# Another order from the planner, and another way to fetch alpha, in a fused attention and two-MLP kernel

## Chip, cores and metric

The kernel runs on one core of a Trainium2 chip, in one launch. The metric is device time in microseconds (us). The engines are named as in the profile: PE (TensorE), PEld (its weight loads), DVE (VectorE), ACT (ScalarE), POOL (GpSimd) and SP (SyncE), which here issues every DMA.

## What is computed

Attention with a forget gate over 4 batches, 8 heads, 576 positions and a head width of 64, then two MLPs over the 2304 resulting rows (512 to 2048 to 512 each). The reference, cut to what matters:

```python
cum = np.cumsum(np.log(np.clip(f, 0.0001, 1.0)), axis=-1)
scores = scale * q @ k.T + (cum[..., :, None] - cum[..., None, :])   # causal
attn = softmax(scores) ; x = attn @ v        # -> (2304, 512)
h = x @ w_in
g = np.maximum(h, 0.0) + alpha * np.minimum(h, 0.0)                  # first MLP
x = g @ w_out
h = x @ moe2_w_in
g = np.maximum(h, 0.0) + np.log1p(np.exp(-np.abs(h)))                # second MLP
return g @ moe2_w_out
```

`alpha` has one number for each of the 2048 hidden columns.

## The kernel before

**The work.** Two heads of one batch make a pair; there are 16 pairs. A pair is worked in nine query tiles (four of each head, and one with the last 64 rows of both). For a tile, POOL writes the decay into `d`, PE writes scores into PSUM (`pt`, L621 or L634), DVE adds them and takes the row maximum (L643), ACT takes the exponential into `p` (L651), PE turns `p` over (L660), ACT and DVE split the result into a high and a low part (L681, L685), and PE multiplies it with the values (L725). `row_sums` sends the row sums by way of DRAM (`rd`, L781) and back as a broadcast (`rb`, L786, L790).

**The MLPs** are split into items of 384 rows (a chunk) by 512 hidden columns. Each item has four times `hidden` (12 matmuls, L889, and the nonlinearity on ACT and DVE, with `slope` holding minus alpha at L902) and the `product` (12 matmuls in each of four groups, L946). Each weight block is fetched raw, 512 KB in 64-bit words (`raw`, L386 and L391), and taken apart by ACT and DVE in eight steps that begin with `ca` on ACT (L394); blocks that are needed again are saved to DRAM (`w_dh`, `w_dl`, L438).

**Stages.** The first eight pairs run with twice the buffers and PE has no MLP work beside them. Then `switch1` gives half of the space to the first MLP: its twelve items on chunks 0 to 2 are mixed with pairs 8 to 15. The rows of those pairs go to DRAM (`xb_dh`, `xb_dl`, L817) and come back after `switch2` as chunks 3 to 5 (`x3h`, `x3l` and so on, L849). From there on PE has only MLP work.

**What sets the order.** Every step is given to `Plan` with an engine, a length, what it reads and writes, and a rank. `Plan.emit` plays the steps through with these lengths and, whenever an engine is free, takes the ready step of the lowest rank. The order in which it takes them is the order in which the instructions are written; on the chip each engine then goes through its own list in that order and waits where an operand is not there. So the lengths only decide the order, and an error in them shows as a wait. `hop` is the allowance from one engine to the next, `late` what a transfer adds to the transfer clock, and `TUNE` has the offsets of the ranks, in steps of a query tile or of an MLP block: two numbers for a step of the attention (first and second eight pairs), one for a step of the MLPs.

Of the kernel before, what the change touches and what calls it, by code (L numbers as in the profile page):

```python
# [14 lines left out]
ALU = mybir.AluOpType  # L15
# [3 lines left out]


TUNE = {
    "TILE1": 0.42, "TILE2": 0.47, "SLOT2": 7.65, "SLOT3": 13.68, "qr": (-5.98, -0.1), "kr": (0.68, -0.52),
    "vr": (-1.32, 560.85), "cum": (11.69, 8.14), "q": (-1.09, -699.23), "k": (-3.93, -2.73),
    "v": (8.47, 0.66), "decay": (-1.18, 0.77), "scores": (0.88, 3.13), "max": (-8.47, 0.3),
    "pad": (-25.9, 9.39), "exp": (79.74, 1.39), "turn": (-0.12, -0.34), "hi": (1.38, 0.0),
    "lo": (2.49, -2.45), "values0": (16.5, 0.87), "values1": (148.3, 515.38), "sum": (3.42, -0.84),
    "finish": (-1.52, 37.07), "sums": (-1.34, -5.25), "blocks": 6.2, "product": 14.59, "total": 1.13,
    "weights": -0.99, "raw": -0.0, "mlp": -1.66,
}


class Plan:
# [7 lines left out]
    @staticmethod  # L40
    def hop(a, b):

        if a == b:
            return {"pe": 0.0, "dve": 0.13}.get(a, 0.1)
        if b == "act":
            return 0.2
        return {"pe": 0.11, "pool": 0.17, "dve": 0.29 if a == "pe" else 0.15}.get(b, 0.1)
# [33 lines left out]
    def emit(self):  # L81
        ops, place = self.ops, self.place
# [47 lines left out]
        while done < len(ops):  # L130
            moved = True
            while moved:
                moved = False
                for e in engines:
                    if free[e] > now + 1e-9:
                        continue
                    best, got = None, None
                    for n in waiting[e]:
                        if ops[n][9] and port_at > now + 1e-9:
                            continue  # L140
                        if can[n] <= now + self.LOOK and (best is None or ops[n][5] < ops[best][5]):
                            g = get_room(n)
                            if g is not None:
                                best, got = n, g
                    if best is None or can[best] > now + 1e-9:
                        continue
                    waiting[e].remove(best)
                    for key, x in got.items():
                        place[key] = x
                        room[key[0]].remove(x)  # L150
                        for line in (key[0], key[:2]):
                            if line in self.queue:
                                served[line] += 1
                    free[e] = now + ops[best][1]
                    end = free[e]
                    if ops[best][9]:
                        port_at = end
                    if e == "sp":
                        moved_at = max(now + 1.2, moved_at) + ops[best][6]
                        moved_at = max(moved_at, end + 0.6 + ops[best][6] / 2)  # L160
                        end = moved_at + 0.95
                    running.append((end, best))
                    order.append(best)
                    moved = True
            times = [t for t, _ in running] + [can[n] for e in engines for n in waiting[e] if can[n] > now + 1e-9]
            times += [t for t in (port_at, *free.values()) if t > now + 1e-9]
            assert times, [sorted([(ops[n][5], ops[n][4]) for n in waiting[e]], key=str)[:3] for e in engines]
            now = min(times + [t for t, _ in leaving])
            for t, key in [x for x in leaving if x[0] <= now + 1e-9]:
                leaving.remove((t, key))  # L170
                room[key[0]].append(place[key])
            for t, n in [r for r in running if r[0] <= now + 1e-9]:
                running.remove((t, n))
                done += 1
                for tag, ids in (ops[n][7] or {}).items():
                    room[tag].extend(ids)
                for key in uses[n]:
                    pending[key] -= 1
                    if not pending[key]:
                        leaving.append((t + 0.2, key))  # L180
                for m in after[n]:
                    left[m] -= 1
                    hop = 0.0 if ops[n][0] == "sp" else self.hop(ops[n][0], ops[m][0])
                    can[m] = max(can.get(m, 0.0), t + hop)
                    if not left[m]:
                        waiting[ops[m][0]].append(m)
# [30 lines left out]
def forgetting_attention_two_mlps(  # L217
# [18 lines left out]
    nc = tc.nc  # L236
# [12 lines left out]
    NFF = DFF // 128  # L249
# [5 lines left out]
    NU = len(UNITS)  # L255
    SWITCH = len(pairs) // 2

    plan = Plan(
        {
            "qr": [0], "kr": [0], "vr": [0], "cumb": [0, 1], "q": [0], "k": [0], "qw": [0, 1], "kw": [0, 1], "v": [0, 1],  # L260
            "d": [0, 1, 2, 3], "p": [0, 1, 2, 3], "mx": [0, 1, 2, 3], "sm": [0, 1], "xt0": [0], "xt1": [0], "x32": [0, 1], "r": [0],
            "rd": [0, 1], "rb": [0], "pt": list(range(8)), "ahead": [0, 1, 2, 3],
            **{"P%d%d%d" % (t, x, n): [0] for t in range(len(UNITS)) for x in range(2) for n in range(2)},
            "raw": [0, 1], "ca": [0, 1], "cu": [0, 1], "win": list(range(5)),
            "wout": [], "h": [], "o": [], "g": [], "ta": [],
        },
# [7 lines left out]
    TILE1, TILE2, SLOT2, SLOT3 = (TUNE[x] for x in ("TILE1", "TILE2", "SLOT2", "SLOT3"))  # L274
    DUE = TUNE
    T_HALF = TILE1 * SWITCH * NU

    def R(n):

        return n * TILE1 if n < SWITCH * NU else T_HALF + (n - SWITCH * NU) * TILE2  # L280
# [15 lines left out]
    ident = const.tile([128, 128], F32, name="ident")  # L296
# [5 lines left out]
    slope = const.tile([128, NFF], F32, name="slope")  # L302
# [14 lines left out]
    def buf(key):  # L317
        return tiles[key[0], plan.place[key]]
# [43 lines left out]
    def weights(kind, m, ff, key, rank):  # L362
# [13 lines left out]
        rkey, ua, uu = ("raw", key), ("ca", key), ("cu", key)  # L376
# [43 lines left out]
            nc.vector.scalar_tensor_tensor(out=buf(key)[1], in0=buf(ua), scalar=2.0 ** -52, in1=buf(uu).bitcast(F32),  # L420
                                           op0=ALU.mult, op1=ALU.mult)

        plan.add("sp", 0.65, load, reads=[("begun", 1)], writes=[rkey], rank=rank + DUE["raw"], late=1.46)
        plan.add("act", t_act(512), lower, reads=[rkey], writes=[ua], rank=rank)
        plan.add("dve", t_dve(512, True), shift, reads=[ua], writes=[uu], rank=rank, port=True)
        plan.add("dve", t_dve(512), join, reads=[rkey], writes=[uu], rank=rank, port=True)
# [578 lines left out]
    with tc.manual_schedule():  # L1005
# [142 lines left out]

        for i in range(SWITCH):
            pair(i)  # L1150
        plan.add("sp", 0.5, lambda: nc.sync.dma_start(out=slope, in_=alpha.rearrange("(k p) -> p k", p=128)),
                 reads=[("y", 0, 0, 0)], writes=[("alpha",)], rank=60, late=0.2)
        plan.add("dve", 0.1, lambda: nc.vector.tensor_scalar(out=slope, in0=slope, scalar1=-1.0, scalar2=None, op0=ALU.mult),
                 writes=[("alpha",)], rank=60)

        plan.add("switch", 0.0, switch1, reads=plan.everything(), writes=[("switch1",)], rank=0.0,
                 grow={"wout": range(5), "g": range(6), "ta": range(2), "h": range(2), "o": range(2)})
# [54 lines left out]
```

## Time and profile before

| | |
|---|---|
| median of 3 runs | 1038.0 us (1037.36 to 1039.97) |
| time of the profiled execution | 1037.31 us |
| its span in the trace | 1035.1 us |
| busy in the span: PE, DVE, ACT, POOL | 1022.3, 725.1, 518.5, 240.3 us |
| HBM read and written | 78.66 MB, 22.17 MB |
| mean granted clock of TensorE | 0.995 of full |

The profiled execution's time is 2.2 us more than its span. PE's busy time counts overlapping matmuls once, so its gaps are real waits; but a busy PE may still be slowed, by a lower granted clock or by a short wait that the end of the matmul before covers.

### The profile page before, as it was taken

To read this page: it belongs to the slowest core of one execution; us is meant where nothing else is said; L and a number is where in the kernel's file an instruction comes from. 1 tells how busy PE (TensorE), PEld (TensorE's weight loads), DVE (VectorE), ACT (ScalarE), POOL (GpSimd) and SP (SyncE) were. 2 spreads that over 40 slices of the span, in tenths; PEclk is the share of its full clock that TensorE was granted. 3 is DMA by queue.
4 is the path that set the end of the run, shared out by engine and by line. 5 is a ranking of instruction groups with operands and counts; after the bars stand their busy time and mean duration, and the time that the engine had idled before them with its cause. 6 is when DMAs were issued, how large, how long until landed. Compare 5 with 4: busy or idle time off the path is not lost.

```text
span 1035.1 us, 17156 instructions
## 1 busy us (share of the span) xinstructions
PE 1022.3 (99%) x6023; PEld 946.4 (91%) x6023; DVE 725.1 (70%) x1605; ACT 518.5 (50%) x1264; POOL 240.3 (23%) x399
## 2 busy tenths in 40 slices
PE   8899999999999999999999999999999999999998
PEld 6678899999999899999999999999999998999997
DVE  5898789979999988532335488738765885685543
ACT  6778777776767655344333354434522332332221
POOL 7677766355566520000000000000000000000000
PEclk8999999999999999999999999999999999999999
DMA  7676446646654248020412221202110211010102
GB/s 185 158 225 176 106 124 198 196 147 184 198 167 144 92 159 288 18 71 32 142 40 84 82 61 34 69 1 82 39 45 1 82 41 42 1 41 1 61 31 91
DMA packets 114021, 101.94 MB, mean 98 GB/s; under 512 B 66624, under 2 KB 87248, under 8 KB 113936
## 3 DMA queue, kind: packets, MB, share of 16 engines
q1 hardware_dynamic: 113936, 100.86, 32.3%
q8 instruction: 47, 0.77, 0.3%
q14 instruction: 38, 0.31, 0.1%
HBM read 78.66 MB, written 22.17 MB: 97 GB/s over the span
## 4 chain that ended last, share of the span: by engine, by line
PE 81%; DVE 7%; ACT 4%; issue 3%; POOL 3%; DMA 2%; POOLq 0%; ACTq 0%; DVEq 0%; SPq 0%
PE o L946 36%; PE h L889 35%; PE pt L725 3%; PE pt L621 3%; PE pt L660 2%; POOL d L599 2%; ACT p L651 1%; PE pt L508 1%; DVE d L643 1%; DMA raw<-in_moe_w_in_dram 1%; PE pt L634 1%; DVE p01l L685 1%; DVE ca L409 1%; DVE g L928 1%; DVE acc L967 1%
## 5 line engine op out<-in xcount | busy, mean ns | idle before, releaser
L946 PE MATMUL o<-g,wout 128*128 128x384 f32 x1152 | 213.6, 337 | 0.0
L946 PE MATMUL o<-wout,g 128*128 128x512 f32 x864 | 205.2, 391 | 0.0
L946 PEld LDWEIGHTS o<-g,wout 128*128 128x128 f32 x1152 | 199.4, 188 | 2.3 <-issue 1.9
L946 PEld LDWEIGHTS o<-wout,g 128*128 128x128 f32 x864 | 161.5, 188 | 32.0
L925 ACT CAST g<-h 128x384 fp32r<-128x384 f32 x192 | 92.2, 481 | 141.4 <-PE o L946 126.7
L928 DVE TENSOR_TENSOR g<-h,g 128x384 fp32r<-128x384 f32 x192 | 106.2, 554 | 80.6 <-ACT g L925 79.8
L599 POOL TENSOR_SCALAR d<-cumb,cumc 64x576 f32<-64x576 f32 (+4 forms) x160 | 117.8, 740 | 96.2 <-ACT p L651 90.9
L915 ACT ACTIVATE ta<-ta 128x384 f32<-128x384 f32 x96 | 50.4, 525 | 135.5 <-DVE ta L911 135.2
L902 DVE SCALAR_TENSOR_TENSOR h<-ta,slope,h 128x384 f32<-128x384 f32 x96 | 58.9, 613 | 73.6 <-ACT h L899 73.4
L651 ACT ACTIVATE p<-d,mx 128x128 f32<-128x128 f32 (+2 forms) x144 | 84.4, 588 | 25.8 <-DVE mx L643 24.8
L896 ACT ACTIVATE ta<-h 128x384 f32<-128x384 f32 x96 | 47.3, 492 | 95.2 <-PE h L889 94.6
L911 DVE TENSOR_SCALAR ta<-h 128x384 uint32<-128x384 uint32 x96 | 53.3, 555 | 39.5 <-PE h L889 39.5
L918 DVE SCALAR_TENSOR_TENSOR h<-h,ta 128x384 f32<-128x384 f32 x96 | 54.2, 564 | 38.1 <-ACT ta L915 37.9
L643 DVE CUSTOM_DVE_ANT_0 d<-pt,d 128x128 f32<-128x128 f32 (+2 forms) x144 | 65.3, 477 | 9.7 <-PE pt L626 4.6
L967 DVE TENSOR_TENSOR acc<-o,acc 128x512 f32<-128x512 f32 (+1 forms) x102 | 60.3, 621 | 16.8 <-PE o L946 16.6
L660 PE MATMUL pt<-ident,p 128*128 128x128 f32 (+1 forms) x400 | 65.1, 281 | 4.7 <-ACT p L651 4.3
L660 PEld LDWEIGHTS pt<-ident,p 128*128 128x128 f32 (+1 forms) x400 | 45.7, 140 | 12.3 <-ACT p L651 7.8
L889 PE MATMUL h<-x1h,win 128*128 128x384 f32 x256 | 54.8, 339 | 0.9 <-DVE g L928 0.9
L889 PE MATMUL h<-x2h,win 128*128 128x384 f32 x256 | 55.3, 340 | 0.1
L394 ACT ACTIVATE ca<-raw 128x512 f32<-128x512 f32 x64 | 43.1, 675 | 24.3 <-DMA raw<-in_moe_w_in_dram 11.6
L889 PE MATMUL h<-x0h,win 128*128 128x384 f32 x256 | 54.9, 339 | 0.3 <-DVE g L928 0.3
L889 PE MATMUL h<-x5h,win 128*128 128x384 f32 x256 | 53.5, 335 | 0.0
(157 smaller groups left out, 1909.8 us busy)
## 6 DMA issues: line engine op xcount, KB each, us to landing
raw<-in_moe_w_in_dram SPq DMA_DIRECT2D x32, 512.0 KB, 3.7
raw<-in_moe_w_out_dram SPq DMA_DIRECT2D x32, 512.0 KB, 3.7
cumb<-cum_d SPq DMA_DIRECT2D x30, 288.0 KB, 4.5
out_dram<-acc SPq DMA_DIRECT2D x18, 256.0 KB, 2.1
qr<-in_q_dram SPq DMA_DIRECT2D x32, 128.0 KB, 2.4
vr<-in_v_dram SPq DMA_DIRECT2D x32, 128.0 KB, 2.9
kr<-in_k_dram SPq DMA_DIRECT2D x32, 128.0 KB, 3.3
rb<-rd SPq DMA_DIRECT2D x32, 128.0 KB, 2.9
```

Of the source, the lines that this page charges most:

```text
L599: nc.gpsimd.tensor_scalar(out=buf(dk)[r, 0:w], in0=buf(cb)[r, hh, 0:w], scalar1=-1.0, scalar2=cumc[r, e, i:i + 1], op0=ALU.mult, op1=ALU.add,)
L643: nc.vector.tensor_tensor_reduce(out=d[:, c0:c1], in0=buf(key)[:, 0:c1 - c0], in1=d[:, c0:c1], scale=-1.0, scalar=least, op0=ALU.add, op1= ...
L651: nc.scalar.activation(out=buf(pk)[:, 0:w], in_=buf(dk)[:, 0:w], func=AF.Exp, bias=buf(mk)[:, x:x + 1], scale=-1.0, accum_out=buf(sm)[:, e ...
L660: nc.tensor.transpose(out=buf(tk[x])[0:rows, (j - j0) * 128:(j - j0) * 128 + 128], in_=buf(pk)[:, j * 128:j * 128 + rows], identity=ident,)
L889: nc.tensor.matmul(out=hb(), lhsT=w_[:, kk * 128:kk * 128 + 128], rhs=x_[:, kk, :], start=(s == 0), stop=(s == len(ops) - 1))
L902: nc.vector.scalar_tensor_tensor(out=hb(), in0=buf(ka), scalar=slope[:, ff:ff + 1], in1=hb(), op0=ALU.mult, op1=ALU.add)
L911: nc.vector.tensor_scalar(out=buf(ka).bitcast(U32), in0=hb().bitcast(U32), scalar1=0x80000000, scalar2=None, op0=ALU.bitwise_or)
L918: nc.vector.scalar_tensor_tensor(out=hb(), in0=hb(), scalar=0.0, in1=buf(ka), op0=ALU.max, op1=ALU.add)
L925: nc.scalar.copy(out=buf(kg)[0], in_=hb())
L928: nc.vector.tensor_sub(buf(kg)[1], hb(), buf(kg)[0].bitcast(F32))
L946: nc.tensor.matmul(out=buf(ok)[:, 0:width], lhsT=a, rhs=b_, start=(j == 0 and s == 0), stop=(j == G - 1 and s == 2))
L967: nc.vector.tensor_add(buf(ok)[:, 0:width] if inner else ac(), buf(ok)[:, 0:width], ac())
```

## The change

The planner's model of transfers is altered: a step that follows a transfer is taken 0.4 later (before: at once), a step on SP is taken 0.8 after the step that it waits for on another engine (before 0.1), and a raw fetch of the first MLP counts 2.6 instead of 1.46 on the transfer clock. All offsets in `TUNE` are other numbers, of which two lines show what they are like. And alpha, before one DMA that put it into `slope` column by column (2048 single numbers), then negated on DVE, is now fetched as 16 rows of 128 into a free `p` buffer, turned over by PE into a free `pt` bank, and copied from there by ACT with a factor of -1. It is placed with the last of the first eight pairs; before, its rank was 60 and it waited for the first attention output.

```diff
-    "TILE1": 0.42, "TILE2": 0.47, "SLOT2": 7.65, "SLOT3": 13.68, "qr": (-5.98, -0.1), "kr": (0.68, -0.52),
...
+    "TILE1": 0.77, "TILE2": 0.39, "SLOT2": 4.51, "SLOT3": 5.11, "qr": (-13.56, 0.57), "kr": (1.29, 0.52),
...
+        if b == "sp":
+            return 0.8
...
-                    hop = 0.0 if ops[n][0] == "sp" else self.hop(ops[n][0], ops[m][0])
+                    hop = 0.4 if ops[n][0] == "sp" else self.hop(ops[n][0], ops[m][0])
...
-        plan.add("sp", 0.65, load, reads=[("begun", 1)], writes=[rkey], rank=rank + DUE["raw"], late=1.46)
+        plan.add("sp", 0.65, load, reads=[("begun", 1)], writes=[rkey], rank=rank + DUE["raw"], late=1.46 if m else 2.6)
...
-        plan.add("sp", 0.5, lambda: nc.sync.dma_start(out=slope, in_=alpha.rearrange("(k p) -> p k", p=128)),
-                 reads=[("y", 0, 0, 0)], writes=[("alpha",)], rank=60, late=0.2)
-        plan.add("dve", 0.1, lambda: nc.vector.tensor_scalar(out=slope, in0=slope, scalar1=-1.0, scalar2=None, op0=ALU.mult),
-                 writes=[("alpha",)], rank=60)
+        AK, AP_ = ("p", "alpha"), ("pt", "alpha")
+        plan.add("sp", 0.5, lambda: nc.sync.dma_start(out=buf(AK)[0:NFF, 0:128], in_=alpha.rearrange("(k p) -> k p", p=128)),
+                 writes=[AK], rank=R(NU * (SWITCH - 1)), late=0.2)
+        plan.add("pe", 0.15, lambda: nc.tensor.transpose(out=buf(AP_)[:, 0:NFF], in_=buf(AK)[0:NFF, 0:128], identity=ident[0:NFF, 0:NFF]),
+                 reads=[AK, ("ident",)], writes=[AP_], rank=R(NU * (SWITCH - 1)))
+        plan.add("act", 0.1, lambda: nc.scalar.mul(out=slope, in_=buf(AP_)[:, 0:NFF], mul=-1.0),
+                 reads=[AP_], writes=[("alpha",)], rank=R(NU * (SWITCH - 1)))
```

**What moves, at three places.** In the changed program the same statements stand two lines further down (L388 is the raw fetch that was L386, L396 the `ca` that was L394, and so on).

The first place is the start of pair 2 on ACT, around the third `ca` (the first step on the third raw block). Before:

```order
L651 ACTIVATE p_0_152,sm_0_133<-d_0_149,mx_0_132 128x128
L778 ACTIVATE r_0_137<-pt_0_119 9x128
L681 CAST p11h<-pt_0_159 128x3x2x64
L681 CAST p00h<-pt_0_120 128x2x64
L681 CAST p00h<-pt_0_158 128x2x64
L520 COPY kw_0_164<-pt_0_119 128x256
L394 ACTIVATE ca_0_87<-raw_0_85 128x512
L651 ACTIVATE p_0_112,sm_0_133<-d_0_150,mx_0_129 128x576
```

and now, from the same 576-wide exponential on:

```order
L653 ACTIVATE p_0_112,sm_0_133<-d_0_150,mx_0_129 128x576
L683 CAST p00h<-pt_0_121 128x2x64
L544 ACTIVATE qw_0_162<-pt_0_119 128x256
L544 ACTIVATE qw_0_162<-pt_0_118 128x320
L522 COPY kw_0_164<-pt_0_157 128x256
L522 COPY kw_0_164<-pt_0_160 128x320
L653 ACTIVATE p_0_113,sm_0_133<-d_0_110,mx_0_130 128x256
L653 ACTIVATE p_0_151,sm_0_133<-d_0_111,mx_0_131 128x256
L683 CAST p00h<-pt_0_121 128x4x64
L415 CAST win_0_93<-cu_0_90 128x512
L653 ACTIVATE p_0_152,sm_0_133<-d_0_149,mx_0_132 128x512
L683 CAST p00h<-pt_0_157 128x4x64
```

One more 512-wide exponential follows these twelve rows, and then the `ca`: it stood directly ahead of the 576-wide exponential and now stands thirteen rows behind it.

The second place is alpha. On SP its fetch stood behind the third raw fetch and ahead of the first save. Before:

```order
L500 DMA cumb_0_146<-cum_d 128x576 x2
L386 DMA raw_0_85<-in_moe_w_in_dram 128x4x128
L1151 DMA slope<-in_moe_alpha_dram 128x16x1
L438 DMA w_dh<-win_0_91 128x512
L438 DMA w_dl<-win_1_92 128x512
L781 DMA rd_0_139<-r_0_137 9x128
L386 DMA raw_0_86<-in_moe_w_in_dram 128x4x128
```

Now nothing stands between the raw fetch and the save, and alpha comes some eighty rows later, behind a `kr` fetch (of pair 9):

```order
L482 DMA vr_0_128<-in_v_dram 128x4x64 x2
L486 DMA vr_0_128<-in_v_dram 64x2x64
L482 DMA kr_0_127<-in_k_dram 128x4x64 x2
L486 DMA kr_0_127<-in_k_dram 64x2x64
L1154 DMA p_0_112<-in_moe_alpha_dram 16x128
L788 DMA rb_0_136<-rd_0_138 64x512
```

On PE its transposition now stands at the end of the values of pair 6, ahead of a turn of pair 8:

```order
L727 MATMUL pt_0_120<-p01h,v_0_108 128x192
L727 MATMUL pt_0_120<-p01h,v_0_108 128x64
L727 MATMUL pt_0_120<-p01l,v_0_108 128x64
L727 MATMUL pt_0_120<-p01h,v_0_108 128x64
L1156 MATMUL pt_0_158<-ident,p_0_112 128x16
L662 MATMUL pt_0_119<-ident,p_0_113 128x128
```

The buffer `p_0_112` that alpha lands in is freed by a turn on PE; between that turn and alpha's transposition stand 10 other transpositions of 128 rows, 6 score matmuls of 288 columns and the 15 matmuls of a values step. So PE, which never waited for alpha's fetch, now does where the fetch is not there in time.

The third place is the fetch of chunks 3 to 5 on SP, behind the last store of the attention (`xb_dl`). Before:

```order
L817 DMA xb_dh<-rb_0_136 128x576
L817 DMA xb_dl<-x_0_109 128x576
L372 DMA win_0_4987<-w_dh 128x512
L372 DMA win_1_4988<-w_dl 128x512
L849 DMA x3h<-xb_dh 128x4x384
L849 DMA x4h<-xb_dh 128x4x192 x2
L849 DMA x5h<-xb_dh 128x4x384
L372 DMA wout_0_1972<-w_dh 128x512
L372 DMA wout_1_1973<-w_dl 128x512
L372 DMA wout_0_4989<-w_dh 128x512
L372 DMA wout_1_4990<-w_dl 128x512
L386 DMA raw_0_86<-in_moe_w_in_dram 128x4x128
```

and now:

```order
L819 DMA xb_dh<-rb_0_136 128x576
L819 DMA xb_dl<-x_0_109 128x576
L388 DMA raw_0_86<-in_moe_w_in_dram 128x4x128
L374 DMA win_0_5109<-w_dh 128x512
L374 DMA win_1_5110<-w_dl 128x512
L851 DMA x3h<-xb_dh 128x4x384
L851 DMA x4h<-xb_dh 128x4x192 x2
L851 DMA x5h<-xb_dh 128x4x384
L374 DMA wout_0_5111<-w_dh 128x512
L374 DMA wout_1_5112<-w_dl 128x512
L851 DMA x3l<-xb_dl 128x4x384
```

Before, `x3l` is the next row after those shown. On PE there stood 22 groups of 12 MLP matmuls between the last attention matmul and the first on chunk 3; now there are 15, since seven more groups are mixed into the attention (77 instead of 70). Behind the first matmul on chunk 3 the order on PE is as before.

## Rows read from the trace of the kernel before

**Rows 1.** Busy time in stretches: length, busy and count by engine, clock, DMA share, GB/s

```profile
core 0: us, PE busy (x) PEld busy (x) DVE busy (x) ACT busy (x) POOL busy (x), PEclk, DMA share, GB/s
0.00:15.00 15.00, 12.36 (x58) 9.49 (x60) 6.58 (x22) 5.73 (x15) 11.91 (x36) 0.78 0.60 149
...
41.60:44.40 2.80, 0.08 (x4) 0.00 (x0) 1.89 (x7) 1.42 (x3) 0.00 (x0) 1.00 0.91 213
44.40:46.00 1.60, 1.59 (x9) 0.90 (x11) 1.44 (x5) 0.90 (x3) 1.46 (x3) 0.99 0.56 129
46.00:49.40 3.40, 3.40 (x19) 1.90 (x15) 3.33 (x9) 2.94 (x10) 3.11 (x4) 0.50 0.57 184
...
60.00:140.00 80.00, 78.80 (x628) 66.97 (x625) 64.81 (x196) 60.63 (x191) 62.68 (x108) 1.00 0.55 149
140.00:380.00 240.00, 237.75 (x1549) 221.74 (x1548) 223.85 (x531) 174.98 (x455) 132.22 (x208) 1.00 0.54 164
380.00:1030.00 650.00, 649.90 (x3468) 614.19 (x3467) 388.72 (x738) 240.95 (x493) 2.86 (x2) 1.00 0.19 60
```

**Rows 2.** The chain that ended last, two pieces: start, length, what

```profile
388.92 10.40 PE h L889 x60
...
1014.88 15.02 PE o L946 x66
```

**Rows 3.** Timeline of PE, 38 to 52 us: start, length, instruction, idle before it

```profile
37.95 0.84 PE L660 MATMUL pt<-ident,p 128*128 128x128 f32 x5
38.63 0.42 PE L508 MATMUL pt<-ident,kr 128*128 128x128 f32 x2
38.81 0.39 PE L725 MATMUL pt<-p01h,v 128*128 128x320 f32 x1
...
40.89 0.70 PE L621 MATMUL pt<-kw,qw 64*128 64x256 f32 x4
41.42 0.25 PE L626 MATMUL pt<-maskb,identb 64*128 64x128 bf16 x4
44.41 0.77 PE L660 MATMUL pt<-ident,p 128*128 128x128 f32 x5 [2.73 <-ACT p L651]
...
46.95 0.85 PE L508 MATMUL pt<-ident,kr 128*128 128x128 f32 x3
47.73 1.65 PE L621 MATMUL pt<-kw,qw 64*128 64x384 f32 x4
...
49.45 0.55 PE L508 MATMUL pt<-ident,qr 128*128 128x128 f32 x3
49.84 0.38 PE L660 MATMUL pt<-ident,p 128*128 128x128 f32 x2
```

**Rows 4.** Timeline of ACT around the third `ca`

```profile
39.17 0.40 ACT L520 COPY kw<-pt 128x256 f32<-128x256 f32 x1
42.94 0.66 ACT L394 ACTIVATE ca<-raw 128x512 f32<-128x512 f32 x1 [3.37 <-DMA raw<-in_moe_w_in_dram]
43.51 0.76 ACT L651 ACTIVATE p<-d,mx 128x576 f32<-128x576 f32 x1
...
50.86 0.72 ACT L651 ACTIVATE p<-d,mx 128x512 f32<-128x512 f32 x1
```

**Rows 5.** The chain, 30 to 50 us

```profile
37.26 5.66 DMA raw<-in_moe_w_in_dram
```

**Rows 6.** Timeline of SP's DMA issues around alpha

```profile
37.26 0.38 SPq L386 DMA_DIRECT2D raw<-in_moe_w_in_dram  x1
37.69 0.50 SPq L1151 DMA_DIRECT2D slope<-in_moe_alpha_dram  x1
38.28 4.19 SPq L438 DMA_DIRECT2D w_dh<-win  x1
42.60 0.35 SPq L438 DMA_DIRECT2D w_dl<-win  x1
```

**Rows 7.** The page's DMA issues: KB each, median us to landing

```profile
raw<-in_moe_w_in_dram SPq DMA_DIRECT2D x32, 512.0 KB, 3.7
...
rb<-rd SPq DMA_DIRECT2D x32, 16.0 KB, 2.6
...
slope<-in_moe_alpha_dram SPq DMA_DIRECT2D x1, 8.0 KB, 5.8
```

**Rows 8.** Matmuls kept apart by shape: busy, mean ns of one, idle before

```profile
L775 PE MATMUL pt<-ident,sm 128*9 128x128 f32 x16 | 4.4, 275 | 0.3 <-ACT p L651 0.3
```

**Rows 9.** What PE waited for: total, times, longest

```profile
PE pt L660 <- ACT p L651: 4.3, 4, 2.7
...
PE h L889 <- DVE g L928: 1.2, 3, 0.6
```

**Rows 10.** Timeline of PE at the end of the attention

```profile
378.16 0.28 PE L725 MATMUL pt<-p01l,v 128*128 128x64 f32 x1
378.28 0.94 PE L889 MATMUL h<-x0h,win 128*128 128x384 f32 x4
```

**Rows 11.** The fetches of chunks 3 to 5 (line L849): duration ns, first and last start

```profile
L849 SPq DMA_DIRECT2D x3l<-xb_dl x1: 535/535/535, 398.3 to 398.3; - x1
...
DMA to landing us min/median/max: 8.7/9.1/9.4
```

**Rows 12.** The instructions that read `x3h`: duration ns, first and last start

```profile
L889 PE MATMUL h<-x3h,win x256: 333/334/346, 424.1 to 981.3; 128*128 128x384 f32 x128
```

More of the change, by code (lines that the diff above doesn't have):

```diff
@@ L21 @@
 TUNE = {
-    "TILE1": 0.42, "TILE2": 0.47, "SLOT2": 7.65, "SLOT3": 13.68, "qr": (-5.98, -0.1), "kr": (0.68, -0.52),
[L23 to L28, printed above, removed]
+    "TILE1": 0.77, "TILE2": 0.39, "SLOT2": 4.51, "SLOT3": 5.11, "qr": (-13.56, 0.57), "kr": (1.29, 0.52),
+    "vr": (0.18, -6.31), "cum": (5.58, 3.5), "q": (-1.59, -201.78), "k": (5.06, -1.31), "v": (4.3, 1.32),
+    "decay": (-3.18, 0.7), "scores": (-0.02, -0.43), "max": (-1.42, -8.16), "pad": (13.38, 1.63),
+    "exp": (49.39, -2.01), "turn": (3.63, -5.55), "hi": (-13.23, 1.49), "lo": (2.32, 0.4),
+    "values0": (6.92, 33.6), "values1": (182.4, 238.62), "sum": (118.44, 0.06), "finish": (-31.74, 0.51),
+    "sums": (-0.44, -33.73), "blocks": 6.9, "product": 4.6, "total": 6.48, "weights": -42.65, "raw": 0.77,
+    "mlp": 0.59,
 }
```

## The prediction

> **What bounds the kernel now.** I looked first at busy time in stretches [rows 1]. PE is busy nearly everywhere, so the question is what its gaps and its slow places cost. From 380 us on there is no gap (649.90 of 650.00 us), and the chain that ended last shows PE at one steady rate there: 60 matmuls of 384 columns in 10.40 us, 0.173 us each, and near the end 66 of 512 columns in 15.02 us, 0.228 us each [rows 2]. No order can shorten that; it can only spoil it. Whatever the change brings lies before 380 us, and the same table says how much there is. PE idles 2.64 us in the first 15 us (start and the first dependent tiles, with the clock at 0.78), 2.72 us between 41.6 and 44.4 us, 1.20 us from 60 to 140 us and 2.25 us from 140 to 380 us [rows 1]. [...]
>
> [...] PE's turn of a 576-wide tile comes 2.73 us late, for want of ACT's `p` [rows 3]. ACT had stood still for 3.37 us in front of the third `ca`, waiting for a raw block, and the exponential that PE needs was queued right behind it [rows 4]. The chain gives that raw fetch 5.66 us from its issue at 37.26 us [rows 5]; the usual raw fetch takes 3.7 [rows 7]. On SP the issue next behind it is alpha's fetch in single numbers, and the one after that, a save that elsewhere takes as little as 0.35 us to issue, takes 4.19 us [rows 6]. Alpha's fetch itself takes 5.8 us for 8 KB [rows 7]. So two things made the wait: the fetch was issued only 2 us before ACT came to it, and it was 2 us slower than usual.
>
> **The change part by part**, against the profiled execution's 1037.3 us.
>
> *The raw wait, -4.1 us.* Both causes are touched. Alpha's fetch is gone from behind the raw fetch. And the `ca` now stands thirteen ACT rows behind the 576-wide exponential, no longer ahead of it; in the trace of before the two 512-wide exponentials that now precede it end some 8 us after that exponential's start (43.51 to about 51.5 [rows 4]), of which I count only the thirteen rows at about 0.5 us, 6 us. SP's place of the raw fetch has not moved against its neighbours. So ACT comes to the block 6 us later, and even a fetch of 5.66 us would be there, 3.37 us of wait against 6 us of cover. That takes the 2.72 us of PE. The slow clock that follows is priced step by step: three transpositions take 0.78 us from start to start at 46.95 us and 0.39 at 49.45 us [rows 3], and the group of eight score matmuls at 47.73 us takes 1.72 us; at full clock I put it at half plus what DVE, 98% busy in that stretch [rows 1], would have held it up anyway, 0.9. With the small steps between that is 1.4 us. 2.7 + 1.4 = 4.1 us. Bounds: nothing, if the raw block is as late as before at its new place, and 2.72 + 1.7 = 4.4 us.
>
> [...] The row shows 0.50 behind a gap of 2.72 us and full clock both before and from 49.4 us on [rows 1]. [...]
>
> *The other waits of the first eight pairs, -0.6 us.* I compared the two orders on PE by counting, for each attention step, the PE work that stands between it and the PE step whose result it needs by way of DVE, ACT or POOL. Steps with less than 2.6 us of such cover, from pair 2 on: 11 before, 6 now. The waits there are 1.20 us in all [rows 1]; half of that is 0.6. Bounds: 1.2 us gained, nothing gained. The start is the same step for step, but for two transpositions that now follow each other; nothing there, give or take 0.5.
>
> *The second eight pairs, +0.7 us.* By the same count there are now 18 such closely set steps among the MLP groups, before 11. New kinds are scores set one MLP group (2.08 us) behind the transposition of their own q or k, and the last values. The 11 of before share the 2.25 us of idle time with everything else there [rows 1], at most 0.2 us each. Seven more would be 1.4 us; I take half, since some of that idle time is other waits, such as PE for `g` [rows 9]. Bounds: nothing, since a cover of 2 us mostly sufficed, and 7 x 0.6 = 4.2 us, by the longest wait that an MLP step had in this trace [rows 9]. MLP steps have their covers as before, and the order behind switch2 is the same from chunk 3 on.
>
> *Alpha, +0.2 us.* Removed: a DVE instruction, off PE's path. Added on PE: one small transposition, 0.03 to 0.28 us by the nearest, that of the row sums [rows 8]. ACT's copy lies in ACT's idle time. What counts is that PE now waits for the fetch. The buffer is freed some 4 us of PE work ahead: 15 values matmuls 2.08 us (38.81 to 40.89), 10 transpositions at 0.68 / 5 = 0.14 us (37.95 to 38.63 [rows 3]), 6 scores like values of that width at 0.14. The fetch needs its issue, 0.5 us [rows 6], and a landing like the row sums' 2.6 us [rows 7], 3.1 us. Nearly 1 us is left over; I take 0.2 in all. Bounds: 0.03 us, and 2.7 us, the longest wait PE had for anything behind it on such a chain [rows 9], if SP is held up by the `kr` fetch just ahead. Behind alpha on PE are a turn and values of pairs 8 and 7, on SP the `rb` fetches of pair 6.
>
> *The fetch of chunks 3 to 5, 0.* Before, the last attention matmul was over at 378.28 us [rows 10], `x3l` was issued at 398.3 and landed about 9.1 us later [rows 11], 29.1 us after the attention; the first matmul on chunk 3 began at 424.1 [rows 12]. Now only 15 groups of 2.08 us stand between, 31.2 us, and `x3l` is read 0.7 us after. That leaves 2.8 us. Fewer transfers stand ahead of it now, but the row sums stand closer to the end. I take nothing; bounds 0 and 3 us, all that the fetch would have to slip twice over.
>
> Sum: -4.1 - 0.6 + 0.7 + 0.2 = -3.8 us. The median of the three runs, 1038.0, stands 0.7 above the profiled execution; from it the forecast is **1034 us**.
>
> **Rivals.** (a) *More is won*: the new order also ends the waits in both halves (-1.2 and -2.25) and part of the start's 2.64 us: 1038 - 4.4 - 3.5 - 1 = 1029 us. For it speaks that the allowance is now for just the wait that was seen; against it that half of the attention has more closely set steps. Chance 0.13.
> (b) *The wait only moves*: a raw block, or alpha ahead of PE, is waited for at another place. For alpha: a gap as long as the one at 41.6 us would cost 2.7 us and the slow clock behind it 1.4, and cancel the gain: 1038 us. For it speaks the thin cover of 1 us, against it that alpha's fetch is now 16 rows. With chunk 3 coming late by 3 us it is 1037. Chance together 0.26, no change.
> (c) *Slower*: in the second half the seven new closely set steps wait for ACT and DVE, which have the MLP's work queued in front of theirs. It makes the kernel slower from (3.8 + 3.1) / 7 = 1.0 us for each. For it speaks that DVE is 93% busy there (223.85 of 240 [rows 1]) and a wait of 2.7 us for `p` did occur [rows 9]; against it that the 11 of before cost at most 0.2 us each. At 1.5 us each: 1034 + 10 = 1044 us. Chance 0.11.
> My forecast, a gain between 3.1 and 6 us, has 0.50.
>
> **Numbers.** About 0.3% (3.1 us) is what can be told from no change here. Faster 0.13 + 0.50 = 0.63, same 0.26, slower 0.11. The likeliest case alone is 1032 to 1035 us. To leave out no more than two in ten the range goes down to (a), 1029, and up past (b) to 1039.5, which leaves out most of (c).
>
> **What would show it.** Right: no gap of PE over 1 us between 38 and 60 us, no stretch at half clock there, no ACT wait of over 1 us for `raw` before 100 us; alpha's transposition without a gap ahead of it; idle time of PE from 140 to 380 us at 2 to 4 us; no gap before the first matmul on `x3h`, and the last 600 us as before. Wrong: a gap on PE with ACT's `p` or DVE's q and k named as releaser in the second half, a gap ahead of L1156, a new stretch at half clock, or any gap behind switch2.

## The result and the profile after

The changed kernel takes **1045.2 us** (median of 4 runs, 1044.3 to 1046.6) against 1037.9 for the kernel before beside it: ratio 1.0079, 95% interval [1.0064, 1.0093]. It is slower by 6.6 to 9.7 us, where 1034 was forecast. Its profiled execution spans 1043.4 us (1035.1 before).

Busy time in stretches, changed kernel, columns as in [rows 1]:

```profile
0.00:15.00 15.00, 12.38 (x56) 9.22 (x56) 6.30 (x22) 5.90 (x15) 11.76 (x36) 0.77 0.62 151
15.00:40.00 25.00, 23.72 (x179) 17.26 (x177) 21.09 (x66) 21.26 (x67) 16.32 (x28) 0.93 0.65 167
40.00:60.00 20.00, 19.46 (x148) 14.88 (x147) 19.41 (x61) 16.82 (x52) 13.87 (x22) 1.00 0.74 201
60.00:140.00 80.00, 79.36 (x627) 67.74 (x627) 62.82 (x189) 58.07 (x183) 61.65 (x103) 1.00 0.56 152
140.00:200.00 60.00, 56.89 (x362) 51.12 (x362) 54.64 (x131) 46.27 (x124) 31.15 (x56) 1.00 0.51 153
200.00:260.00 60.00, 58.14 (x366) 55.33 (x366) 51.03 (x113) 38.48 (x94) 19.84 (x31) 1.00 0.58 178
260.00:320.00 60.00, 58.76 (x388) 55.33 (x387) 57.30 (x129) 42.65 (x111) 36.99 (x55) 1.00 0.59 178
320.00:380.00 60.00, 58.50 (x385) 53.51 (x384) 56.58 (x136) 40.67 (x108) 32.64 (x55) 1.00 0.42 132
...
430.00:1030.00 600.00, 600.00 (x3192) 565.77 (x3191) 356.51 (x678) 220.71 (x449) 0.00 (x0) 1.00 0.16 50
```

Between 40 and 60 us the long gap and the half rate are gone (PE busy 19.46 of 20 us, clock 1.00). But from 140 to 380 us PE now idles 3.11 + 1.86 + 1.24 + 1.50 = 7.7 us, before 2.25 [rows 1], and the last 600 us are untouched.

Two instructions mark off nearly equal work in either order: the first product of the first MLP on `x0h` and the first on `x3h`. Between them lie three chunks of that MLP and the second eight pairs but for a few of their first steps (1788 of PE's matmuls here, 1791 before). Timeline of PE, changed kernel:

```profile
142.94 0.96 PE L891 MATMUL h<-x0h,win 128*128 128x384 f32 x4
...
432.28 0.85 PE L891 MATMUL h<-x3h,win 128*128 128x384 f32 x4
```

That is 289.3 us. Before, the same two gave 282.5:

```profile
141.65 0.95 PE L889 MATMUL h<-x0h,win 128*128 128x384 f32 x4
...
424.12 0.85 PE L889 MATMUL h<-x3h,win 128*128 128x384 f32 x4
```

So **6.9 us are lost in the second half**. The first half, in which the forecast saw its gain, ends 1.3 us later; in these two executions alone that is not clear of the spread that the last section tells of. What PE waited for up to 400 us (total, times, longest):

```profile
PE pt L662 <- ACT p L653: 3.2, 5, 1.0
PE pt L777 <- DVE p01l L687: 1.7, 1, 1.7
...
PE h L891 <- DVE g L930: 1.3, 2, 0.8
PE pt L510 <- DVE mx L645: 1.1, 3, 0.5
PE o L948 <- DVE wout L422: 0.8, 1, 0.8
```

The one wait of 2.7 us for `p` [rows 9] is gone; in its place stand many of up to 1.7 us.

### The profile page after: what moved, and what is told of

It reads as the page before. It is cut to its first block, busy times and chain, and to the rows that moved or that the text cites. A ratio compares the mean times of both kernels' runs of the same rounds, so it can differ in the third digit from the quotient of the medians.

```text
span 1043.4 us, 17153 instructions
## 1 busy us (share of the span) xinstructions
PE 1025.8 (98%) x6024; PEld 945.4 (91%) x6024; DVE 730.2 (70%) x1604; ACT 518.4 (50%) x1265; POOL 235.8 (23%) x399
## 4 chain that ended last, share of the span: by engine, by line
PE 82%; DVE 8%; POOL 3%; issue 3%; ACT 2%; DMA 1%; SPq 0%; POOLq 0%; DVEq 0%; ACTq 0%
PE o L948 36%; PE h L891 36%; PE pt L727 3%; PE pt L662 3%; PE pt L623 3%; PE pt L510 1%; DVE d L645 1%; POOL d L601 1%; PE pt L636 1%; DVE ca L411 1%; DVE p01l L687 1%; ACT p L653 1%; POOL v L581 1%; DVE h L904 1%; DMA vr<-in_v_dram 1%
## 5 line engine op out<-in xcount | busy, mean ns | idle before, releaser
L601 POOL TENSOR_SCALAR d<-cumb,cumc 128x128 f32<-128x128 f32 (+4 forms) x160 | 107.8, 676 | 109.4 <-ACT p L653 95.9
L891 PE MATMUL h<-x3h,win 128*128 128x384 f32 x256 | 53.3, 335 | 0.0
```

Source lines behind the costliest of these rows:

```text
L601: nc.gpsimd.tensor_scalar(out=buf(dk)[r, 0:w], in0=buf(cb)[r, hh, 0:w], scalar1=-1.0, scalar2=cumc[r, e, i:i + 1], op0=ALU.mult, op1=ALU.add,)
L891: nc.tensor.matmul(out=hb(), lhsT=w_[:, kk * 128:kk * 128 + 128], rhs=x_[:, kk, :], start=(s == 0), stop=(s == len(ops) - 1))
```

## The experiments

Theory 1 was that the new order of the second eight pairs makes PE wait for a crowded VectorE. Its rivals: single steps of PE set too close, whatever VectorE does; alpha's new form; the first half; or the new numbers, wherever they act. (A step is *closely set* where little other work of PE stands between it and the step whose result it needs.) I give times with the ratio to the kernel before on the same chip, and *h to x3* for the stretch between the two marks, which the kernel before's order of that stretch repeats to 0.2 us (282.3 to 282.5 in seven kernels that keep it). The changed kernel's 1045.2 us were not measured beside these runs, so differences from it in us are rough; the ratios compare better.

**Alpha alone**, in the order of before.

```diff
-        plan.add("sp", 0.5, lambda: nc.sync.dma_start(out=slope, in_=alpha.rearrange("(k p) -> p k", p=128)),
...
+            nc.tensor.transpose(out=t, in_=arow, identity=ident[0:NFF, 0:NFF])
+            nc.vector.tensor_scalar(out=slope, in0=t, scalar1=-1.0, scalar2=None, op0=ALU.mult)
+
+        plan.add("sp", 0.5, lambda: nc.sync.dma_start(out=arow, in_=alpha.rearrange("(k p) -> k p", p=128)),
```

> The kernel before, its order kept word for word, with alpha alone changed: fetched in rows into a tile of its own at the same place on SP, transposed by TensorE right behind the product y(1,0,0), and negated by VectorE. If the slow fetch of alpha (4.19 us for the descriptors of its neighbour, rows 6) held up the raw fetches behind it and was what ACT waited for at 44.41 us: the 2.73 us gap of TensorE, its half-rate stretch at 46.0 to 49.4 us or both shrink, and the time comes to 1034 to 1036 us. If the raw fetch was late for another reason: within 0.5 us of 1038 us. If the new form of alpha itself costs (TensorE waiting for rows or for a tile): 1039 us or more, with a gap at the transposition.

Measured 1038.9 us, 1.0013 [0.9997, 1.0028]. Its timeline of SP, and of ACT at the third `ca`:

```profile
37.49 0.38 SPq L389 DMA_DIRECT2D raw<-in_moe_w_in_dram  x1
37.92 0.49 SPq L1161 DMA_DIRECT2D arow<-in_moe_alpha_dram  x1
38.51 0.37 SPq L441 DMA_DIRECT2D w_dh<-win  x1
...
43.55 0.66 ACT L397 ACTIVATE ca<-raw 128x512 f32<-128x512 f32 x1 [3.27 <-DMA raw<-in_moe_w_in_dram]
```

The neighbour's issue falls from 4.19 us [rows 6] to 0.37, so alpha's single numbers did hold up SP. But ACT still waits 3.27 us for the raw block (before 3.37 [rows 4]). Alpha's fetch was not what made it late.

**No fetch of alpha** (`slope` filled by a memset).

> The kernel before, its order kept, with alpha not fetched at all: the tile of slopes is filled with the constant -1.2 by VectorE, so the output is not the reference's. It bounds from below what any form of fetching alpha can give: 1034 to 1036 us if alpha's fetch is behind the wait at 44.41 us, about 1038 us if it is not.

Measured 1038.2 us, 0.9994 [0.9981, 1.0008]: no gain from any form of that fetch can be told from the noise. In its profile ACT waits for the same raw block even longer, 4.51 us.

**VectorE's load**, in both orders: two of VectorE's six steps on a weight block of the first MLP left out.

```diff
         def join():
+            if m == 0 and (kind, part) != (0, 0):
+                return
...
         def power():
+            if m == 0 and (kind, part) != (0, 0):
+                return
```

> The changed kernel, its order kept, with two of VectorE's four steps on each weight block of the first MLP left out (joining the sign and the powers of two, about 1.15 us of a block, some 25 blocks; the weights are then wrong, the kernel computes something else). Theory 1, the second eight pairs of the new order wait for a VectorE that is filled to about 95%: the stretch from 140 to 400 us gives back most of its loss, 1045 comes down by 5 to 8 us to 1037 to 1040. Theory 2, the steps stand too close for the latency from engine to engine whatever VectorE has to do: under 2 us come back, 1043 us or more.

> The kernel before with the same steps of VectorE left out (the weights are then wrong). Its TensorE waits in the second eight pairs are short, so theory 1 expects less from it than from the changed kernel: 1 to 3 us, 1035 to 1037 us. If it comes down as far as the changed kernel does, VectorE's load weighs on both alike and is no reason for the difference between the two.

Measured 1038.8 us (1.0009 [0.9995, 1.0024]) for the changed order, 1035.7 (0.9974 [0.9961, 0.9988]) for that of before: 6.4 and 2.4 us less than with the steps. *h to x3* falls from 289.3 to 283.5 and from 282.5 to 279.4. Theory 1 holds in the size of both gains, with the closely set steps left as they were; but of the 6.9 us between the orders about 4 still stand.

**Half of the order each.** In these kernels a written list of the steps takes the place of the planner's choice: the changed order up to the switch between the halves and the old one behind it, and the reverse.

```diff
-                    if best is None or can[best] > now + 1e-9:
-                        continue
...
+        done, todo = set(), list(LIST)
```

> The changed kernel, its own order kept word for word up to the end of the first eight pairs (with alpha in rows and TensorE's transposition), and behind that point the order of the kernel before. Theory 1, the loss lies in the order of the second eight pairs alone: 1037 to 1039 us, and TensorE's busy time from 140 to 380 us as in rows 1 (about 237.8 of 240 us). Theory 2, the loss comes from the first half or from alpha's new form, which leave the second half late: 1043 us or more. Theory 3, the first half alone is a gain hidden by the second: 1034 us, as forecast.

> The kernel before, its order kept up to the end of the first eight pairs (alpha in its old form), and behind that point the order of the changed kernel. Theory 1: 1044 to 1046 us, the whole loss, with the single waits of the changed kernel behind 140 us (for p01l, wout and ACT's p, together about 7 us of TensorE). Theory 2: within 1 us of 1038 us.

Measured 1038.7 us (1.0013 [0.9995, 1.003]) and 1045.3 us (1.0073 [1.0047, 1.0099]). Stretches of the first kernel, columns as above:

```profile
15.00:40.00 25.00, 23.34 (x182) 16.86 (x177) 21.86 (x68) 21.85 (x69) 16.46 (x28) 0.97 0.73 184
40.00:60.00 20.00, 19.84 (x153) 15.77 (x152) 19.53 (x60) 17.41 (x55) 14.80 (x24) 1.00 0.71 193
200.00:260.00 60.00, 59.38 (x390) 56.64 (x388) 52.72 (x120) 41.59 (x108) 31.37 (x50) 1.00 0.60 184
```

And two of the second, where PE's time is short as in the changed kernel:

```profile
140.00:200.00 60.00, 57.03 (x359) 51.25 (x360) 54.56 (x130) 44.84 (x120) 28.27 (x52) 1.00 0.53 151
200.00:260.00 60.00, 58.14 (x357) 55.70 (x357) 49.81 (x111) 37.95 (x94) 19.00 (x32) 0.97 0.56 178
```

The loss goes with the second half's order (*h to x3* 290.8 us), and not with the first half's or alpha's form (282.5). Of the 290.8, up to 1.8 us are the clock's, by an estimate: the 0.97 above (1.00 in the changed kernel) is what 3.6 of the 60 us at a clock of 0.50 would give, half of them lost. The first half shows no gain either: of the 2.6 us of busy PE that it wins at 40 to 60 us, 1.6 are missing at 15 to 40 us. The same stretches of the kernel before:

```profile
15.00:40.00 25.00, 24.94 (x197) 19.70 (x198) 22.21 (x69) 22.88 (x73) 17.47 (x28) 1.00 0.64 170
40.00:60.00 20.00, 17.27 (x129) 13.64 (x129) 17.00 (x52) 13.35 (x40) 13.12 (x20) 0.91 0.75 208
```

**The parts through the planner**: alpha's new form with the old numbers, and the new numbers with the old form.

> The numbers of the kernel before with the changed kernel's form of alpha alone; the planner makes its order anew from that. By order's rows the order of the second eight pairs then differs from that of the kernel before, though none of its numbers do, with 17 products set close to their predecessors' step, as in the changed kernel's 18. Theory 1 with the addition that the count of closely set steps is the measure: 1043 to 1046 us. Theory 4, every redrawn order is a draw of its own and the numbers alone don't say which way: anything from 1036 to 1046 us, with TensorE's loss again between 140 and 400 us. If alpha's form costs nothing and the order of the second half does not matter: 1038 us.

> The changed kernel's numbers, hop costs and slack for transfers, with alpha in its old form; the planner makes its order anew, and that differs again. If alpha's new form is what costs 7 us: 1036 to 1039 us. If the numbers of the second eight pairs cost them, with alpha of no account: 1043 to 1047 us. By the count of closely set steps (21 against 18): 1045 us or more.

Measured 1048.3 us (1.0101 [1.0073, 1.0129]) and 1050.4 (1.0116 [1.0083, 1.0149]), the first above every time that was expected for it. Both are slower than before; the medians are also above that of the changed kernel, which has both parts, but the intervals overlap; *h to x3* is 288.5 and 289.6 us, and the rest of their time lies ahead of the first mark (147.48 and 148.77 us, the changed kernel 142.94). Alpha's new form alone, one small step more and on other engines, makes the planner redraw the order of a half where nothing was changed, and the redrawn one costs 6.0 us there, nearly what the new numbers cost.

Whether the count of closely set steps measures the loss stays open. With 11 of them *h to x3* is 282.5 us, with 17 288.5, with 18 289.3, with 21 289.6. But the last of these has a lower granted clock in two stretches, where the others have 1.00. Two rows of the new numbers with the old form:

```profile
140.00:200.00 60.00, 55.68 (x356) 49.77 (x355) 53.35 (x134) 44.81 (x122) 35.48 (x64) 0.97 0.51 154
...
380.00:400.00 20.00, 17.91 (x104) 17.14 (x103) 14.52 (x30) 10.99 (x27) 4.11 (x6) 0.91 0.36 114
```

Each is what 3.6 us at a clock of 0.50 would give, half of them lost, so that by this estimate up to 3.6 us of its 7.1 are the clock's, and what is left is less than the 6.9 of 18 such steps.

**The forecast's main term alone**, one step on ACT (and its reader on DVE) in the order of before; then the same wait from SP's side. Rows of the order, ACT:

```diff
-L340 ACTIVATE ca_0_87<-raw_0_85 128x512
 L597 ACTIVATE p_0_112,sm_0_133<-d_0_150,mx_0_129 128x576
 L627 CAST p01h<-pt_0_157 128x4x128
 L627 CAST p01h<-pt_0_159 64x128
+L340 ACTIVATE ca_0_87<-raw_0_85 128x512
```

and SP:

```diff
+L332 DMA raw_0_85<-in_moe_w_in_dram 128x4x128
 L426 DMA kr_0_127<-in_k_dram 128x4x64 x2
 L430 DMA kr_0_127<-in_k_dram 64x2x64
 L446 DMA cumb_0_146<-cum_d 128x576 x2
-L332 DMA raw_0_85<-in_moe_w_in_dram 128x4x128
```

> The kernel before with one step moved: ACT's first step on the third weight block (the ca that waited 3.37 us for its raw, rows 4) behind the 576-wide exp and its two casts, and VectorE's step that reads it behind the differences of the same casts; nothing else. This is the forecast's main term alone. As the forecast had it: the 2.73 us gap of TensorE and the half-rate stretch behind it go, 1033.5 to 1035.5 us. Rival: TensorE arrives earlier at waits that follow (for VectorE or ACT), and most is given back before 140 us: 1037 to 1038.5 us, with the first product of the first MLP within 1 us of its time in the kernel before less what the start differs.

> The kernel before with one step moved on SP: the fetch of the third raw block ahead of the three issues of kr and the two of cumb, some 4.4 us earlier, when its tile has just come free (32.98 us). ACT keeps its order. If the late fetch is the whole cause of the wait: it lands by about 39 us, the gap goes as with the later ca, 1033.5 to 1035.5 us. If the queues' bandwidth there is the limit, the fetches of k and cumb land later by what raw took, and a wait for kr or the cumulated sums takes the place of the gap: 1037 to 1039 us.

Measured 1035.3 us (0.9978 [0.9966, 0.999]) and 1036.2 (0.998 [0.9967, 0.9993]). ACT's timeline with the later `ca`:

```profile
41.09 0.78 ACT L597 ACTIVATE p<-d,mx 128x576 f32<-128x576 f32 x1 [1.46 <-DVE mx L589]
41.77 0.19 ACT L597 ACTIVATION_READ_ACCUMULATOR p<-d,mx 128x1 f32 x1
42.71 0.74 ACT L627 CAST p01h<-pt 128x512 fp32r<-128x512 f32 x2 [0.75 <-PE pt L606]
43.35 0.67 ACT L340 ACTIVATE ca<-raw 128x512 f32<-128x512 f32 x1
```

The exponential starts at 41.09 us instead of 43.51 [rows 4] and the block is there when ACT comes to it. The first MLP begins at 138.7 us instead of 141.65; but this execution has half rate at the start for 3.4 us (clock 0.50 from about 13 to 16.4 us), the kernel before's for 6.8 (8.4 to 15.2), and how much of the difference that makes isn't shown. With the earlier fetch ACT has no wait for the block either, but PE gets a new one of 1.1 us for `qr`. Both versions beat the kernel before and the changed one; the later `ca` is worth about 2.3 us in the median.

**Single stops of PE filled**, in the changed order: four steps of PE that were ready go ahead of the one that waits, at three places (`val` is an attention product with the values, `h` and `o` a group of MLP matmuls, `turn` the transposition of a tile of `p`).

```diff
+val x(9,0)
 h(2,0)
-val x(9,0)
...
+h(7,1)
 turn 119
-h(7,1)
...
+o(8,0)
 turn 137
-o(8,0)
```

> The changed kernel, its order kept, with four steps of TensorE moved by one or two places in the second half: at three of its stops (185, 314 and 376 us in its trace, 0.91, 0.52 and 1.03 us lost) a product that was ready (two products of attention with v, one group of h, one of o) goes ahead of the step that waits. If these stops are only steps that stand too close: 2 to 2.5 us come back, 1042.7 to 1043.2 us. If VectorE's and ScalarE's queues set the pace there, TensorE meets them a step later: under 0.7 us, 1044.5 us or more.

Measured 1047.6 us, 1.0093 [1.0074, 1.0112]; *h to x3* 291.3, 2.0 more than in the changed kernel. At 185 and 376 us the stops are gone, but others are longer (PE's timeline, three stretches):

```profile
195.66 0.44 PE L608 MATMUL pt<-ident,p 128*128 128x128 f32 x2 [0.88 <-ACT p L599]
...
319.40 0.44 PE L608 MATMUL pt<-ident,p 128*128 128x128 f32 x2 [1.06 <-ACT p L599]
320.51 0.98 PE L837 MATMUL h<-x1h,win 128*128 128x384 f32 x4 [0.68 <-DVE g L876]
...
388.71 0.44 PE L608 MATMUL pt<-ident,p 128*128 128x128 f32 x2 [0.94 <-ACT p L599]
```

In the changed kernel the step at 195.5 us waited 0.29 us and the one at 386.6 none. PE meets the queues a step or two later, as expected where they set the pace. Why it is 2.0 us more isn't shown.

**GpSimd's overlap.** One cluster of stops of PE in the changed kernel (0.75, 0.22 and 0.44 us, from 173 to 177 us) starts with a weight block. VectorE's timeline of the changed kernel:

```profile
170.31 0.69 DVE L411 SCALAR_TENSOR_TENSOR ca<-ca,raw 128x512 f32<-128x512 uint32 x1
170.92 1.65 DVE L399 TENSOR_SCALAR cu<-ca 128x512 uint32<-128x512 uint32 x1
172.50 1.56 DVE L422 SCALAR_TENSOR_TENSOR wout<-ca,cu 128x512 fp32r<-128x512 f32 x1
174.08 0.49 DVE L548 SCALAR_TENSOR_TENSOR q<-pt,q 128x320 fp32r<-128x320 f32 x1
```

GpSimd's timeline of the same stretch:

```profile
170.36 1.92 POOL L806 TENSOR_TENSOR x<-x,rb 128x576 f32<-128x576 f32 x1 [0.64 <-DVE x L761]
172.26 0.41 POOL L565 TENSOR_SCALAR q<-q 64x64 fp32r<-64x64 f32 x1
172.64 0.86 POOL L581 TENSOR_TENSOR v<-vr,v 128x320 fp32r<-128x320 f32 x1
```

The step L399 takes 1.65 us beside GpSimd's product; the same step took 0.43 us at 43.63 us in the kernel before, with GpSimd idle (0.00 us busy from 41.6 to 44.4 [rows 1]), and has a median of 0.42 us in either kernel. PE's `o` waits 0.75 us for the `wout` that comes out at the end. So two steps of GpSimd on each of the second eight pairs were left out, in both orders.

```diff
         def mul():
+            if b >= B // 2:
+                return
             y = buf(yk).bitcast(F32)
...
             def keep_lo():
-                nc.gpsimd.tensor_sub(buf(yk), buf(yk).bitcast(F32), buf(bk).bitcast(F32))
+                return
```

> The changed kernel, its order kept, with two of GpSimd's steps on each of the second eight pairs left out (the scaling of x by the row sums and the low part of x, 16 instructions of about 1.5 us; the output is then not the reference's). In its trace VectorE's six steps on a weight block between 143 and 399 us take about 17 us more than the same steps take with GpSimd idle (the second step 1.65 us at 170.92 instead of 0.41), against 12 us in the kernel before. Theory 1b, GpSimd stretches VectorE and so the wait for a weight block or for p: the stretch shrinks by 5 to 8 us of VectorE's time, the stop of o at 171 us (1.04 us) goes, and 2 to 4 us come back: 1041 to 1043 us. If the stretching is harmless: under 1 us, 1044.2 us or more.

> The kernel before with the same steps of GpSimd left out (the output is then not the reference's). By theory 1b its gain is smaller than the changed kernel's, 0.5 to 1.5 us (1036.5 to 1037.5 us). If both come down alike, GpSimd is not what sets the two orders apart.

Measured 1040.9 us (1.0033 [1.0017, 1.0049]) and 1038.0 (0.9998 [0.9985, 1.0011]): 4.3 us come back in the changed order, 0.1 in the old, less than expected there. *h to x3*: 289.3 to 285.6, and 282.5 to 281.6. Of the cluster at 173 to 177 us one wait of 0.2 us is left. VectorE's groups by line from 143 to 377 us (busy us, mean ns of one), the changed kernel:

```profile
L411 DVE SCALAR_TENSOR_TENSOR ca<-ca,raw 128x512 f32<-128x512 uint32 x23 | 18.7, 813 | 0.2
...
L422 DVE SCALAR_TENSOR_TENSOR wout<-ca,cu 128x512 fp32r<-128x512 f32 x13 | 10.4, 797 | 0.2
L422 DVE SCALAR_TENSOR_TENSOR win<-ca,cu 128x512 fp32r<-128x512 f32 x12 | 9.9, 822 | 0.1
```

The same groups with less of GpSimd's work:

```profile
L411 DVE SCALAR_TENSOR_TENSOR ca<-ca,raw 128x512 f32<-128x512 uint32 x23 | 16.5, 719 | 0.2
...
L422 DVE SCALAR_TENSOR_TENSOR wout<-ca,cu 128x512 fp32r<-128x512 f32 x13 | 9.5, 731 | 0.2
L422 DVE SCALAR_TENSOR_TENSOR win<-ca,cu 128x512 fp32r<-128x512 f32 x12 | 9.0, 749 | 0.1
```

All six steps together are 94.0 us in the changed kernel, 87.0 with less of GpSimd; in the same stretch of the kernel before, with the same number of instructions (144), 90.0 and 85.8. The same work takes VectorE 4.0 us longer in the new order; with less of GpSimd it is 1.2.

**The two parts that had a reason of their own**, the later `ca` and alpha in rows, without the redrawn order.

> The order of the kernel before with the two parts of the change that were meant for a stop of their own and nothing else: the later ca of the third weight block, and alpha in rows transposed by TensorE. If alpha's form is worth nothing once its fetch holds up no one: as with the later ca alone, 1035 to 1035.8 us. If the fetches behind it then land earlier and remove a wait: 1033 to 1034.5 us. If its transposition or its wait for a free tile costs: 1036 us or more.

Measured 1036.9 us, 0.9986 [0.9971, 1.0001] (the kernel before took 1038.1 beside it): not told apart from the later `ca` alone, whose interval it overlaps. A gain from alpha's form isn't shown.

## Why the prediction was wrong

**The step that failed: "The second eight pairs, +0.7 us".** Measured by *h to x3* it is +6.9, beyond its upper bound of 4.2 and as much as rival (c) priced (1044 us, chance 0.11). I took VectorE's 93% [rows 1] as an argument for a rival and not as the limit of that stretch, and priced a closely set step by what the 11 of before had cost, 0.2 us each. The seven more steps came to 1.0 us each, the price at which rival (c) turned the forecast over, instead of the 0.1 that I took. A part of that price is VectorE's load: with two of its steps left out the orders are 4.0 us apart instead of 6.9. Against the single step speaks that filling three stops brought nothing. What sets the two orders apart is shown in part. GpSimd's two steps cost VectorE's weight steps more in the changed order (7.0 us against 4.2); without them *h to x3* is 3.7 us shorter there and 0.8 in the old. The difference, 2.9, is under half of the 6.9, and whether it is the same 2.9 as VectorE's load gave is open. At 170.92 us a step with a median of 0.42 us took 1.65, and it ended, at 172.57 us, just behind a GpSimd product that ends at 172.28 us. By what means GpSimd's work lengthens VectorE's no run shows.

The remaining 4 us stay open. A part of them is a stop at 236 us, where PE waits 1.7 us for `p01l` (1.67 in the changed kernel) in all five kernels with this order of the second half. It doesn't hang on the steps of VectorE or of GpSimd that were left out: without either it is as long. With VectorE's left out, VectorE itself waits there for ACT's cast of `p01h`, and ACT has no gap ahead of that cast from 231.12 to 233.17 us (timelines of VectorE and of PE):

```profile
233.78 1.16 DVE L691 TENSOR_TENSOR p01l<-pt,p01h 128x512 fp32r<-128x512 f32 x2 [0.33 <-ACT p01h L687]
...
234.53 0.28 PE L781 MATMUL pt<-ident,sm 128*9 128x128 f32 x1 [1.67 <-DVE p01l L691]
```

So ScalarE's queue is a rival at this stop, which none of the experiments took away; which rows of the order make the chain from `p` over the casts to the freed tile late I have not separated.

**The raw wait, -4.1 us: right in its place and too large.** Alone it is worth 2.3 us (interval 1.0 to 3.5), about the gap without the 1.4 us for the slow clock. No run shows the 1.7 us in its upper bound of 4.4, and so in rival (a)'s 1029 us: that is half of the 3.40 us at a clock of 0.50 [rows 1], an estimate. With the later `ca` the clock is 1.00 from 40 to 60 us and PE's waits there are 0.6 us at most, and what that brought in all are the 2.3 us. The half rate doesn't follow a gap in every execution: with alpha in rows the same gap, 2.75 us up to 45.02 us, has a granted clock of 1.00 behind it. And from 200 to 260 us, where the changed kernel has the stop of 1.67 us, the granted clock is 0.97 with the old first half and 1.00 in the changed kernel. Of the two causes given for the raw wait one was wrong: alpha's single numbers hold up the issue behind them, not the fetch ahead. Why that fetch takes 2 us more than usual stays open.

**The other waits of the first eight pairs, -0.6 us: wrong in sign.** The changed first half alone comes out at 1.0013 [0.9995, 1.003], the later `ca` alone at 0.9978 [0.9966, 0.999]; if the later `ca` is worth the same in both orders, the rest of that half's new order costs the difference, some 3.6 us. In the profiles of these two, which both have half rate (clock 0.50) from about 13 to 16.4 us, the first MLP begins at 142.72 and 138.71 us, 4.0 apart. Part of it is in the rows above: 1.6 us less of PE's time at 15 to 40 us than the 24.94 that the kernel before shows there, and the later `ca` alone as well. The count of closely set steps, 11 before and 6 now, pointed the other way.

**Alpha, +0.2 us**: no gap ahead of its transposition at 128.2 us; right. **The fetch of chunks 3 to 5, 0**: right; `x3l` was issued at 420.6 us, 12.4 ahead of its use, and PE has no gap there.

Together: -2.3 and +3.6, which are the 1.3 us of the changed first half alone, and +6.9 make 8.2 us, where 6.6 to 9.7 were measured.

## What to carry to other kernels

Where two engines are both filled to over 90% (here PE 99% and VectorE 93% [rows 1]), the gaps that the first shows today are no price for a new order: ask what the second one's load adds, and what its neighbour's does (here 7.0 of the 94.0 us of VectorE's weight steps). A planner's numbers fit the one program that they were found for: one small step more redrew the order of a half that it doesn't touch, and cost 6 us there. When a profile shows one wait with one cause, move the one step and keep the rest of the order: that gave 2.3 us here, and the redrawn order lost it three times over.

## What was not expected of the hardware

At the start TensorE's half rate lasts differently long from execution to execution, though the order there is the same: 6.8 us at a granted clock of 0.50 in the kernel before, 3.4 with the later `ca`, none on record with alpha in rows. And in one execution matmuls were slow with a clock of 1.00 on record. The same eight in PE's timeline, with alpha in rows (clock recorded 1.00):

```profile
6.02 2.44 PE L1098 MATMUL pt<-d,chosen 32*128 32x512 f32 x8
```

And without alpha's fetch, at a recorded 1.00 as well, but nearly twice as long:

```profile
6.02 4.50 PE L1095 MATMUL pt<-d,chosen 32*128 32x512 f32 x8
```

The kernels' times spread by some 6 us from run to run (1034.7 to 1041.0 for the kernel before on one chip). In the profiles the spread lies ahead of the first MLP: in the seven kernels with the old order of the second half that begins at 138.7 to 147.8 us, and the rest of the span is 892.8 to 893.5 us in all of them. So the stretch between two marks behind the start told the orders apart better than the whole time did. How much of the spread the half rate makes isn't shown: with alpha in rows, and no half rate on record, the first MLP began at 141.49 us, no earlier than the 141.65 of the kernel before with 10.2 us of it (6.8 at the start, 3.4 behind the gap). PE then waited more, as for `mx` (3.2 us in all, before 0.2).
